# Moving three gain multiplies and the last-key transposes in the first batch, and respacing batch 1's attention bursts, in a fused attention and feed-forward kernel

## Chip, cores and metric

One core of a Trainium2 chip. The time is the device time of one launch in microseconds (us), lower is better. All runs quoted are fast, with a granted TensorE clock of 0.998 to 1.0. Kernels are compared only with the kernel before in the same rounds on the same chip.

## The reference

```python
def _attn_ref(q, k, v):                      # q, k, v: (8, 12, 448, 64)
    scores = 1/sqrt(64) * q @ k.transpose
    attn = np.maximum(scores, 0.0) ** 2 / 448
    return attn @ v

def _moe_ref(x, g_ln, w_ch1, w_ch2):         # x: (8, 448, 768)
    xn = (x - mean(x)) / sqrt(var(x) + 1e-6) * g_ln
    return x + np.maximum(xn @ w_ch1, 0.0) @ w_ch2      # 768 -> 3072 -> 768
```

Eight batches; 12 heads in 6 pairs per batch, so pairs 0 to 5 are batch 0, 6 to 11 batch 1, 12 to 17 batch 2. The output of attention, transposed, is x.

## The kernel before

TensorE does everything large. A batch's first layer has 24 column blocks of 128; in between them, "bursts" compute three score tiles of the next batch each. The first batch has no earlier first layer to hide in, so its attention runs on its own (`step_fine`), in a pipeline of TensorE (scores), ScalarE (relu out of PSUM), VectorE (square, evictions).

The variance need not be applied before the first layer (it is a factor per token, put in at the end), but the mean must: `xc = x*g - mean*g`. The `ones` matrix holds -1/768, so the mean product gives -mean.

```python
    def av_out(i, ps, evac_by):              # eviction of one pair's attention-value product
        b, pr = divmod(i, NPAIR)
        ...
            nc.vector.tensor_scalar(xT_of(b, pr), ps, c2, None, op0=Alu.mult)          # L362
        ...
        if b == 0:
            if pr < GAIN_FIRST:              # GAIN_FIRST = 3
                nc.vector.tensor_scalar(xc[:, pr, :], xT_of(b, pr), g_sb[:, pr:pr + 1],
                                        None, op0=Alu.mult)                            # L367, the gain multiply
        elif pr == 1: ...                    # sums for the later batches' mean

    def step_fine(i):                        # two pairs of batch 0, i and i + 1
        att_QK(i, 0)                         # scores (L293), then relu on ScalarE (L303)
        att_T(i + 1)                         # transposes of q, k (L229), copy (L268)
        att_square(i, 0)                     # VectorE (L306)
        att_QK(i, 1)
        att_square(i, 1)
        ...warm_up(3)...                     # i == 0 only; products that keep TensorE busy (L600)
        att_QK(i, 2)
        ...
            first_last_keys()                # i == 0: transposes of the last 64 keys of pairs 0, 1; copies (L275)
            warm_up(2)
        att_square(i, 2)
        att_QK(i, NF)                        # last-key product of both pairs (L288)
        ...

    def first_end():                         # i = 6
        att_AV(i - 1, 0); att_QK(i, 0); att_QK(i, 1); att_AV(i - 1, 1)
        mean_part(i - 2)                     # L376
        att_T(i + 1, nc.scalar.copy, next_f())
        mean_part(i - 1)
        att_T(i + 2, nc.scalar.copy, ...)
        # then ffn_1_first: centering of xc 0..2 (L397), first-layer products (L719)

    V_AT = {21: 14, 23: 16}                  # value loads during batch 0's first layer (numbers put in)
    STATS_AT = {0: (18, 21, 23), 1: (10, 14, 17, 22), 2: (2, 5, 8, 14)}
    IN_SECOND = (3, 6, 9, 13, 16, 19, 21)    # column blocks of batch 1 that are followed by a burst

    def queued(i):                           # when pair i's scores are done
        if PE_T * NPAIR <= i + 3 < NP_ALL:
            att_T(i + 3)                     # from pair 12: transpose by DMA, queue SP (L253)
            if i + 6 < NP_ALL:
                loads.append(i + 6)          # its ring slot is reloaded, queue POOL (L169 to L171)
    def excursion(n, ...):                   # a burst
        flush_loads()                        # issues what is in loads
        ...                                  # attention-value products of a finished couple of pairs (L323, L346)
        ...                                  # n scores, relus, squares; queued() for pairs that ended

    # in the loop over column blocks, batch 1: after the third burst the output stores of batch 0's
    # second layer that were held back (L459, 8 DMAs) are issued
                    while ni > bursts[1] and held_stores:
                        held_stores.pop(0)()
```

POOL issues the loads (weights, queries and keys into a ring of three slots, values). SP issues DMA transposes of the ring into `qkT` and the output stores. Both are worked off in program order.

## Time and profile before

| | |
|---|---|
| time | 521.75 us, median of 3 (521.41 to 521.87) |
| profiled execution | span 520.2 us, clock 1.0 |
| TensorE matmul busy | 512.8 us, 99% |
| first batch's first-layer product starts | 29.72 us |
| its second layer starts | 68.73 us |
| last-key product of batch 1's fourth burst | 104.42 us |
| batch 1's second layer starts | 123.31 us |

Busy time on the page's table of engines (engine, busy us, share of the span, instructions):

```profile
PE 512.8 (99%) x5688; PEld 310.4 (60%) x5688; DVE 370.8 (71%) x658; ACT 276.9 (53%) x456; POOL 222.7 (43%) x255
```

The view of waits, TensorE only (who waited, for whom, total us, times, longest):

```profile
PE f L600 <- DVE w L103: 1.2, 1, 1.2
PE sc L288 <- ACT at L303: 0.6, 1, 0.6
PE f L323 <- DVE at L306: 0.4, 2, 0.3
PE f L323 <- DVE xT L362: 0.3, 1, 0.3
...
```

By both, TensorE has almost nothing to win. What they hide is time between starts that is not counted as a wait. The chain of waits (start us, us, what) of the first batch, followed back from the first-layer product:

```profile
10.84 0.63 DVE at L306
11.46 0.54 DVE qkT_t L268
...
13.69 0.58 DVE xc L367
...
16.98 0.60 DVE xc L367
...
20.81 0.40 DVE xc L367
...
27.08 0.55 DVE xT L362
...
27.67 0.35 PE f L376
28.02 0.63 PE f L229 x16
28.65 0.31 PE f L376
...
28.98 0.69 DVE xc L397
...
29.72 0.73 PE f L719 x3
```

For 17 us the chain stays inside VectorE, and three of its members are the gain multiplies (L367), which nobody needs before 28.98 us. ScalarE is close behind, as its relus in the timeline show (start, us, engine, line, operation, count, in brackets the idle time before and what ended it):

```profile
6.83 2.54 ACT L303 ACTIVATE at<-sc 128x896 bf16<-128x896 f32 x3 [0.46 <-PE sc L293]
9.89 9.27 ACT L303 ACTIVATE at<-sc 128x896 bf16<-128x896 f32 x11 [0.52 <-PE sc L288]
19.63 1.85 ACT L303 ACTIVATE at<-sc 128x896 bf16<-128x896 f32 x2 [0.47 <-PE sc L293]
21.73 4.36 ACT L303 ACTIVATE at<-sc 128x896 bf16<-128x896 f32 x5 [0.25 <-DVE at L306]
```

The timeline of TensorE at batch 1's sixth burst (first line: its four last-key products) and at its last burst:

```profile
114.27 0.36 PE L288 MATMUL sc<-qkT_t 64*64 64x448 bf16 x4
...
117.90 0.36 PE L323 MATMUL f<-at,v_ring 128*64 128x448 bf16 x2
118.55 0.38 PE L323 MATMUL f<-at,v_ring 128*64 128x448 bf16 x2 [0.29 <-DVE at L306]
119.09 0.57 PE L323 MATMUL f<-at,v_ring 128*64 128x448 bf16 x4 [0.16 <-DVE at L306]
119.59 0.55 PE L293 MATMUL sc<-qkT_t 64*128 64x448 bf16 x4
...
122.55 0.93 PE L323 MATMUL f<-at,v_ring 128*64 128x448 bf16 x8
123.31 0.98 PE L499 MATMUL f<-w,h 128*64 128x384 bf16 x10
```

Eight attention-value matmuls take 119.59 - 117.90 = 1.69 us from start to next start; three us later eight take 123.31 - 122.55 = 0.76. The bracketed waits add up to 0.45 only; starts show about twice that, because the modelled end of a matmul covers part of the idle time.

The SP queue around batch 1's middle bursts:

```profile
94.72 5.71 SPq L253 DMA_TRANSPOSE qkT_t<-qk_ring  x2
...
102.74 4.37 SPq L459 DMA_DIRECT2D out_dram<-acc_t  x4
107.50 5.26 SPq L253 DMA_TRANSPOSE qkT_t<-qk_ring  x2
```

The first of these is pair 15's transpose (landed 9.4 us after issue, at 104.1), the one at 107.50 is pair 17's (5.4 us, 112.9). These two are needed in the fourth and the sixth burst.

### The profile page before, as it was taken

The page shows a single profiled execution, that of the slowest core. Times are in us where ns is not written, and L with a number is a line of the kernel's source. Part 1 is how long each engine was busy: PE and PEld are TensorE (multiplying, and loading weights), DVE is VectorE, ACT ScalarE, POOL GpSimd, SP SyncE. Part 2 cuts the span into 40 slices and gives each one's busy share as a digit, 9 for nine tenths or more (in the row PEclk, how much of TensorE's full clock was granted, in tenths as well). Part 3 has the DMA queues.
Part 4 walks back from the last instruction along what each step waited for, and adds up shares of the span by engine and source line. Part 5 has one row for each costly group of instructions (what it writes and reads, how often), then busy time and mean ns, then how long its engine had stood idle before and what let it go on. Part 6 is the DMA issues. An engine that isn't in the chain of part 4 may idle for free.

```text
span 520.2 us, 13589 instructions
## 1 busy us (share of the span) xinstructions
PE 512.8 (99%) x5688; PEld 310.4 (60%) x5688; DVE 370.8 (71%) x658; ACT 276.9 (53%) x456; POOL 222.7 (43%) x255
## 2 busy tenths in 40 slices
PE   8999999999999999999999999999999999999996
PEld 4445566555765566655787556655666556665665
DVE  5966779878958769587685868787695866950255
ACT  6976642786247662476624766476524765234320
POOL 8727115688423853238632287238532000320031
PEclk9999999999999999999999999999999999999999
DMA  9999999999436992559934799369923300340022
GB/s 138 190 197 202 183 203 164 138 189 113 79 92 91 117 100 62 122 70 121 83 74 107 73 111 146 75 81 116 89 70 100 62 1 2 74 113 1 1 59 64
DMA packets 175245, 53.01 MB, mean 102 GB/s; under 512 B 154192, under 2 KB 175184, under 8 KB 175184
## 3 DMA queue, kind: packets, MB, share of 16 engines
q0 software_dynamic: 103680, 25.75, 54.5%
q1 hardware_dynamic: 70976, 26.03, 27.5%
q8 instruction: 44, 0.72, 0.6%
q10 hardware_dynamic: 528, 0.37, 0.2%
q14 instruction: 17, 0.14, 0.1%
HBM read 51.91 MB, written 11.01 MB: 121 GB/s over the span
## 4 chain that ended last, share of the span: by engine, by line
PE 93%; DVE 4%; ACT 2%; issue 0%
PE f L431 41%; PE f L499 34%; PE f L323 5%; PE sc L293 4%; PE f L482 3%; DVE at L306 2%; PE f L293 2%; ACT at L303 1%; PE sc L288 1%; PE f L346 1%; PE f L600 1%; PE f L719 1%; DVE xT L362 1%; PE f L229 1%; DVE qkT_t L268 1%; ACT h L433 0%
## 5 line engine op out<-in xcount | busy, mean ns | idle before, releaser
L431 PE MATMUL f<-xc,w 128*64 128x448 bf16 x2256 | 225.6, 353 | 0.1
L431 PEld LDWEIGHTS <-w 128*64 128x64 bf16 x2256 | 125.8, 110 | 91.8 <-issue 13.6
L433 ACT ACTIVATE h<-f 128x448 bf16<-128x448 f32 x188 | 102.7, 546 | 102.5 <-PE f L431 98.0
L499 PE MATMUL f<-w,s_sb 128*64 128x384 bf16 (+2 forms) x1584 | 130.0, 324 | 0.0
L499 PEld LDWEIGHTS <-s_sb 128*64 128x64 bf16 x1584 | 92.7, 110 | 34.4
L303 ACT ACTIVATE at<-sc 128x896 bf16<-128x896 f32 x120 | 103.2, 918 | 5.3 <-PE sc L293 4.4
L306 DVE TENSOR_TENSOR at<-at 128x896 bf16<-128x896 bf16 x168 | 95.5, 617 | 4.8 <-ACT at L303 4.6
L532 POOL TENSOR_TENSOR o_t<-o_t,x_tok 128x384 f32<-128x384 f32 x26 | 24.3, 936 | 149.4 <-ACT o_t L531 149.4
L169 POOL DMA_DIRECT2D qk_ring<-in_q_dram x36 | 46.1, 1282 | 85.6 <-DMA qkT_t<-qk_ring 60.3
L299 DVE TENSOR_SCALAR at<-f 128x448 bf16<-128x448 f32 x89 | 52.6, 619 | 30.7 <-PE f L293 30.7
L531 ACT ACTIVATE o_t<-f,rstd 128x384 f32<-128x384 f32 x26 | 15.1, 581 | 93.5 <-DVE acc_t L536 29.9
L493 DVE TENSOR_TENSOR s_sb<-h 128x1536 bf16<-128x1536 bf16 x65 | 64.1, 1002 | 0.0
L170 POOL DMA_DIRECT2D qk_ring<-in_k_dram x36 | 55.0, 1528 | 12.6 <-DMA w<-in_moe_w_ch_dram 12.6
L499 PE MATMUL f<-w,h 128*64 128x384 bf16 x624 | 52.9, 326 | 0.0
L171 POOL DMA_DIRECT2D qk_ring<-in_k_dram x36 | 46.6, 1294 | 6.4 <-DMA w<-in_moe_w_ch_dram 4.8
L499 PEld LDWEIGHTS <-h 128*64 128x64 bf16 x624 | 36.8, 110 | 14.2
L532 POOL TENSOR_TENSOR acc_t<-acc_t,x_tok 128x384 f32<-128x384 f32 x24 | 28.8, 1209 | 22.3 <-ACT acc_t L531 19.6
L323 PE MATMUL f<-at,v_ring 128*64 128x448 bf16 x288 | 36.5, 357 | 0.8 <-DVE at L306 0.4
L181 POOL DMA_DIRECT2D v_ring<-in_v_dram x36 | 32.8, 1218 | 0.0
L397 DVE SCALAR_TENSOR_TENSOR xc<-f,g_sb,xc 128x448 bf16<-128x448 f32 x45 | 28.5, 677 | 5.4 <-PE f L391 4.6
L362 DVE TENSOR_SCALAR xT<-f 128x448 bf16<-128x448 f32 x33 | 20.3, 617 | 14.3 <-PE f L323 11.3
L293 PE MATMUL sc<-qkT_t 64*128 64x448 bf16 x192 | 30.0, 356 | 0.2 <-DVE qkT_t L268 0.2
(86 smaller groups left out, 392.0 us busy)
## 6 DMA issues: line engine op xcount, KB each, us to landing
w<-in_moe_w_ch_dram POOLq DMA_DIRECT2D x6, 768.0 KB, 12.6
w<-in_moe_w_ch_dram POOLq DMA_DIRECT2D x4, 1152.0 KB, 29.3
v_ring<-in_v_dram POOLq DMA_DIRECT2D x21, 192.0 KB, 5.1
qk_ring<-in_q_dram POOLq DMA_DIRECT2D x36, 112.0 KB, 4.7
qk_ring<-in_k_dram POOLq DMA_DIRECT2D x36, 96.0 KB, 5.1
out_dram<-o_t SPq DMA_DIRECT2D x8, 168.0 KB, 2.2
out_dram<-acc_t SPq DMA_DIRECT2D x7, 168.0 KB, 2.2
out_dram<-o_t SPq DMA_DIRECT2D x8, 144.0 KB, 2.1
```

Of the source, the lines that this page charges most:

```text
L170: nc.gpsimd.dma_start(k_to[:, :NF], k[b, heads, :SF].rearrange("x (p t) d -> p t x d", t=NF))
L171: nc.gpsimd.dma_start(k_to[:SS, NF], k[b, 2 * a:2 * a + 2, SF:].rearrange("x s d -> s x d"))
L293: nc.tensor.matmul(by_j(half[hh]), k_of(i, r, t, P), q_of(i, r), start=True, stop=True)
L299: nc.vector.tensor_scalar(at[:, x], half[x], 0.0, None, op0=Alu.max)
L303: nc.scalar.activation(at, ps[:, :, :S], Act.Relu)
L306: nc.vector.tensor_mul(attn[i, t], attn[i, t], attn[i, t])
L323: nc.tensor.matmul(ps[hh * D:(hh + 1) * D, :], weights, values, start=start, stop=stop)
L431: nc.tensor.matmul(ps[c * D:(c + 1) * D, :], w1[:, ki, n0:n0 + D], xc[:, ki, :], start=(ki == 0), stop=(ki == K1 - 1))
L433: nc.scalar.activation(h[:, ni, CARRY:], ps, Act.Relu)
L493: nc.vector.tensor_tensor(s_sb[:, n], x, y, op=op)
L499: nc.tensor.matmul(ps[c * D:(c + 1) * D, :d1 - d0], stat[:, ki, c * D:(c + 1) * D], w2[:, slot, ki, d0:d1], start=(start and ki == 0), sto ...
L532: nc.gpsimd.tensor_tensor(o_t, o_t, x_half(m, dh), op=Alu.add)
```

## The change

The intent: take the gain multiplies out of VectorE's chain and do them where VectorE waits for the last mean product; bring the last-key product of the first pairs forward; give batch 1's last burst three column blocks of distance instead of two.

```diff
@@ av_out
         if b == 0:
-            if pr < GAIN_FIRST:
-                nc.vector.tensor_scalar(xc[:, pr, :], xT_of(b, pr), g_sb[:, pr:pr + 1], None, op0=Alu.mult)
-        elif pr == 1:
+            return
+        if pr == 1:
@@ step_fine
         att_QK(i, 1)
+        if i == 0:
+            first_last_keys()
         att_square(i, 1)
@@
         else:
-            first_last_keys()
-            warm_up(2)
+            warm_up(3)
@@ first_end
         att_AV(i - 1, 1)
+        att_T(i + 1, nc.scalar.copy, next_f())
         mean_part(i - 2)
-        att_T(i + 1, nc.scalar.copy, next_f())
         mean_part(i - 1)
+        for ki in range(GAIN_FIRST):
+            nc.vector.tensor_scalar(xc[:, ki, :], xT_of(0, ki), g_sb[:, ki:ki + 1], None, op0=Alu.mult)
         att_T(i + 2, nc.scalar.copy, sc_turn.items[-1][:, 0])
@@
-    STATS_AT = {0: (18, 21, 23), 1: (10, 14, 17, 22), 2: (2, 5, 8, 14)}
-    IN_SECOND = (3, 6, 9, 13, 16, 19, 21)
+    STATS_AT = {0: (18, 21, 23), 1: (10, 16, 19, 22), 2: (2, 5, 8, 14)}
+    IN_SECOND = (3, 6, 9, 13, 15, 18, 21)
```

## The prediction

> **What bounds the kernel.** TensorE: the table of engines gives matmuls 512.8 of 520.2 us, granted clock 1.0; the list of waits gives TensorE only 2.9 us. The Trainium skill ("Perfetto Trace Analysis", opening note) calls matmul busy time a bad metric for pipelined matmuls; this trace agrees, since lost time hides inside "busy" groups, so I read starts in the timeline. From 42 us on TensorE runs nearly back to back. Two places lose time:
>
> 1. First batch's attention, 9 to 30 us. The chain of waits runs through VectorE almost without a gap from 10.84 to 27.62 us, and holds three gain multiplies (0.58, 0.60, 0.40 = 1.58 us). ScalarE is nearly full too: relus without a break from 9.89 to 19.16 us, then idle 0.47 and 0.25 until 26.09. Before that, the first last-key product waits for its copies (9.13 us), starts at 9.37, and leaves ScalarE idle 0.52 us.
> 2. Batch 1's last burst, two column blocks after the one before. Its 8 attention-value matmuls take 117.90 to 119.59 = 1.69 us; elsewhere eight take 0.75. Loss 0.94 us, to VectorE's squares.
>
> **What the change does.**
> - Last-key transposes one square earlier: copies at about 8.5 us, product at about 8.9, relu at about 9.4, 0.5 us earlier. The added warm-up matmul fills idle time. The keys land at 7.6 us (3.2 + 4.4), close to the new use at 7.5: may cost 0.1 to 0.2.
> - Gains out of VectorE's chain: up to 1.5 us there, but ScalarE then limits: its last relu can end about 1.2 us earlier (0.52 + 0.47 + 0.25).
> - Gains put back behind the last eviction, 0.33 to 0.5 us each, 1.0 to 1.3 us, of which 0.8 was idle waiting for the mean. VectorE, not the mean, then releases the centering. Net, the first-layer product starts 0.8 to 1.3 us earlier (before: 29.72).
> - Batch 1's bursts at 13, 15, 18, 21: three blocks before the last, and the short gap where no attention-value product follows. The 0.94 us stall should vanish.
>
> **How much survives.** The early microsecond meets a DMA chain that computation does not pace: second-layer weights land at 79.3 us (needed at about 80.6), release the ring's last query/key load, then transposes in one queue. Pair 15's is issued at 94.72, lands 9.4 us later, at 104.1; its product starts at 104.4 to 104.6. So only about 0.3 us of slack is left: I expect TensorE to arrive early and wait 0.5 to 0.9 us there. The next (pair 17, 107.50 + 5.4 = 112.9) is also needed near 113. Gain: 0.94 + about 0.3 = about 1.2 us.
>
> **Predicted: 520.5 us, 8 in 10 between 519.6 and 521.2.** Faster by over 2%: 0.005; within 2%: 0.99; slower by over 2%: 0.005.
>
> **Signs.** Right: last-key product near 8.9 us; no gain multiply before 26 us, three in a row behind the last eviction; first-layer product near 28.6 us; a new TensorE wait on pair 15's transpose just before 105 us, after which the shift is only about 0.3 us; batch 1's last burst's eight matmuls in 0.75 us; everything after it about 1.2 us early. Wrong: first-layer product at 29.5 us or later; a stall at block 15 or 18.
>
> **What would make it wrong.** If transposes move earlier with computation, the gain reaches 2.1 us. If the gains take over 0.5 us each, or pair 17's transpose stalls the moved burst, it falls to 0.5. DMA landings are of one profiled run, and may move by half a microsecond.

## The result, and the profile after

Measured: 520.97 us, median of 4 (519.58 to 521.56), against 521.81 us, median of 4, of the kernel before. The ratio is 0.9981, 95% interval 0.9960 to 1.0002; a ratio is the mean time of one kernel's fast runs over that of the other's of the same rounds, so it is not quite the ratio of the medians. In five further rounds of the same kernel (below) it was 0.9971 (0.9959 to 0.9983). So the change gains 1.0 to 1.5 us of 522, well within 2%. The first interval includes 1 and the second does not: that there is a gain at all rests on the repeat. The profiled execution took 520.69 us (before: 521.98).

In the lines of after, source lines have moved by one or two (L431 is L430, L499 is L498, L719 is L721), and the multiplies are L708. Engines and TensorE's waits:

```profile
PE 511.8 (99%) x5689; PEld 306.5 (59%) x5689; DVE 370.4 (71%) x658; ACT 276.8 (53%) x456; POOL 222.6 (43%) x255
```

```profile
PE f L599 <- DVE w L103: 1.2, 1, 1.2
PE sc L288 <- DMA qkT_t<-qk_ring: 0.8, 1, 0.8
PE f L229 <- DMA w<-in_k_dram: 0.4, 1, 0.4
PE f L229 <- DVE xT L362: 0.2, 1, 0.2
```

The waits for other engines (L303, L306) are gone, and two waits for DMAs have come. The timeline of the first batch: ScalarE's relus, and VectorE's and TensorE's end of the stage.

```profile
6.83 1.73 ACT L303 ACTIVATE at<-sc 128x896 bf16<-128x896 f32 x2 [0.46 <-PE sc L293]
9.03 15.86 ACT L303 ACTIVATE at<-sc 128x896 bf16<-128x896 f32 x19 [0.47 <-PE sc L293]
```

```profile
25.46 1.18 DVE L362 TENSOR_SCALAR xT<-f 128x448 bf16<-128x448 f32 x2
26.56 0.82 DVE L708 TENSOR_SCALAR xc<-xT,g_sb 128x448 bf16<-128x448 bf16 x3
27.36 1.87 DVE L396 SCALAR_TENSOR_TENSOR xc<-f,g_sb,xc 128x448 bf16<-128x448 f32 x3
```

```profile
8.01 0.25 PE L229 MATMUL f<-identity,w 64*64 64x64 bf16 x4 [0.43 <-DMA w<-in_k_dram]
...
9.35 0.38 PE L288 MATMUL sc<-qkT_t 64*64 64x448 bf16 x4
...
28.10 0.73 PE L721 MATMUL f<-xc,w 128*128 128x448 bf16 x3
```

The 19 relus from the third on now run without a break, and the last ends at 24.90 instead of 26.09 us. The three multiplies stand in a row behind the last eviction and take 0.82 us together. The first-layer product starts at 28.10 instead of 29.72: 1.62 us earlier. The last-key product is not earlier (9.35, before 9.37): its transposes waited for the load of the keys.

TensorE at the sixth and seventh burst of batch 1, and the SP queue that serves it:

```profile
111.53 0.35 PE L288 MATMUL sc<-qkT_t 64*64 64x448 bf16 x2
112.73 0.38 PE L288 MATMUL sc<-qkT_t 64*64 64x448 bf16 x2 [0.85 <-DMA qkT_t<-qk_ring]
113.04 0.36 PE L293 MATMUL sc<-qkT_t 64*128 64x448 bf16 x2
...
117.52 0.92 PE L323 MATMUL f<-at,v_ring 128*64 128x448 bf16 x8
118.38 0.55 PE L293 MATMUL sc<-qkT_t 64*128 64x448 bf16 x4
```

```profile
94.37 5.36 SPq L253 DMA_TRANSPOSE qkT_t<-qk_ring  x2
...
101.99 2.73 SPq L458 DMA_DIRECT2D out_dram<-acc_t  x4
105.50 5.70 SPq L253 DMA_TRANSPOSE qkT_t<-qk_ring  x2
```

The last burst's eight matmuls take 0.86 us instead of 1.69: that stall is gone. In its place the four last-key products of the sixth burst are torn apart. The first two are of pair 16, the other two of pair 17, and pair 17's transpose, issued at 105.50, landed 7.2 us later, at 112.7.

The kernel between these places runs at a fixed pace, so marks in the timeline give an exact account. From the mark at batch 1's second layer to the end it is 396.9 us before and 396.8 after.

| us | before | after | difference |
|---|---|---|---|
| start to first-layer product | 29.72 | 28.10 | -1.62 |
| from there to the fourth burst's last-key product (104.42, 102.82) | 74.70 | 74.72 | +0.02 |
| from there to batch 1's second layer (123.31, 122.10) | 18.89 | 19.28 | +0.39 |
| rest of the span | 396.9 | 396.8 | -0.1 |

So 1.62 us won in the first batch arrive in full at the fourth burst, and the third line, where the respacing should win about 0.9, loses 0.4.

### The profile page after: what moved, and what is told of

Its sections match the earlier page's. It is cut to its first block, busy times and chain, and to the rows that moved or that the text cites. A ratio compares the mean times of both kernels' runs of the same rounds, so it can differ in the third digit from the quotient of the medians.

```text
span 518.9 us, 13591 instructions
## 1 busy us (share of the span) xinstructions
PE 511.8 (99%) x5689; PEld 306.5 (59%) x5689; DVE 370.4 (71%) x658; ACT 276.8 (53%) x456; POOL 222.6 (43%) x255
## 4 chain that ended last, share of the span: by engine, by line
PE 91%; DVE 3%; DMA 2%; ACT 2%; POOL 0%; issue 0%; POOLq 0%; ACTq 0%
PE f L430 40%; PE f L498 34%; PE f L323 5%; PE sc L293 4%; PE f L481 3%; PE f L293 2%; DVE at L306 1%; ACT at L303 1%; DMA qkT_t<-qk_ring 1%; PE sc L288 1%; DMA w<-in_k_dram 1%; PE f L346 1%; PE f L721 1%; DVE xT L362 1%; DVE qkT_t L268 0%; ACT h L432 0%
## 5 line engine op out<-in xcount | busy, mean ns | idle before, releaser
L430 PE MATMUL f<-xc,w 128*64 128x448 bf16 x2256 | 225.5, 353 | 0.1
L430 PEld LDWEIGHTS <-w 128*64 128x64 bf16 x2256 | 125.9, 110 | 91.6 <-issue 13.6
L432 ACT ACTIVATE h<-f 128x448 bf16<-128x448 f32 x188 | 102.8, 547 | 102.5 <-PE f L430 97.6
L498 PE MATMUL f<-w,s_sb 128*64 128x384 bf16 (+2 forms) x1584 | 130.0, 324 | 0.0
L498 PEld LDWEIGHTS <-s_sb 128*64 128x64 bf16 x1584 | 90.0, 110 | 37.2
L303 ACT ACTIVATE at<-sc 128x896 bf16<-128x896 f32 x120 | 102.8, 918 | 5.1 <-PE sc L293 4.2
L306 DVE TENSOR_TENSOR at<-at 128x896 bf16<-128x896 bf16 x168 | 95.6, 618 | 4.9 <-ACT at L303 4.7
L498 PE MATMUL f<-w,h 128*64 128x384 bf16 x624 | 52.9, 326 | 0.0
L498 PEld LDWEIGHTS <-h 128*64 128x64 bf16 x624 | 35.7, 110 | 15.3
```

Of the source, the lines that this page charges most:

```text
L303: nc.scalar.activation(at, ps[:, :, :S], Act.Relu)
L306: nc.vector.tensor_mul(attn[i, t], attn[i, t], attn[i, t])
L430: nc.tensor.matmul(ps[c * D:(c + 1) * D, :], w1[:, ki, n0:n0 + D], xc[:, ki, :], start=(ki == 0), stop=(ki == K1 - 1))
L432: nc.scalar.activation(h[:, ni, CARRY:], ps, Act.Relu)
L498: nc.tensor.matmul(ps[c * D:(c + 1) * D, :d1 - d0], stat[:, ki, c * D:(c + 1) * D], w2[:, slot, ki, d0:d1], start=(start and ki == 0), sto ...
```

## The experiments

Theory T, formed from this: TensorE comes early to batch 1, and there meets DMA landings that computation does not pace; the sixth burst, moved one block up, is the one that hits pair 17's. Its main rivals: the wait in that one profile is an accident and the parts simply add; or the wait is the respacing's own doing.

Twelve runs were made, in three groups of four on three chips, 5 rounds each (c_bursts has six executions); all gave correct results. Times and ratios against before of the same rounds, and the marks of each profile:

| run | time, us | ratio (95%) | first-layer product | to 4th burst | to 2nd layer of batch 1 |
|---|---|---|---|---|---|
| before (first profile) | | | 29.72 | 74.70 | 18.89 |
| after (first profile) | | | 28.10 | 74.72 | 19.28 |
| a_after | 520.35 | 0.9971 (0.9959-0.9983) | 28.46 | 75.15 | 18.22 |
| b_first | 520.74 | 0.9977 (0.9965-0.9989) | 27.98 | 74.72 | 19.04 |
| c_bursts | 520.67 | 0.9984 (0.9971-0.9997) | 29.15 | 74.70 | 18.07 |
| d_loads | 520.31 | 0.9975 (0.9962-0.9988) | 27.78 | 75.18 | 18.29 |
| d_both | 519.93 | 0.9963 (0.9950-0.9975) | 28.45 | 74.94 | 18.07 |
| e_gain | 521.26 | 0.9987 (0.9975-1.0000) | 28.18 | 75.43 | 18.89 |
| f_keys | 522.07 | 1.0005 (0.9992-1.0019) | 29.59 | 74.70 | 18.88 |
| g_split | 520.76 | 0.9978 (0.9966-0.9991) | 28.94 | 74.91 | 18.06 |
| d_both_2 | 520.95 | 0.9971 (0.9958-0.9983) | 28.66 | 75.70 | 18.06 |
| h_nokeys | 520.82 | 0.9969 (0.9956-0.9981) | 28.15 | 75.44 | 18.07 |
| d_stores | 520.03 | 0.9956 (0.9944-0.9969) | 28.27 | 74.90 | 18.06 |
| b_first_both | 521.64 | 0.9983 (0.9969-0.9996) | 29.55 | 74.76 | 18.88 |

Read the last two columns first. Undisturbed, "to 4th burst" is 74.70 to 74.72 in every profile, and "to 2nd layer" is 18.88 or 18.89 with the old places of the bursts and 18.06 or 18.07 with the new ones. What stands above is a wait. For "to 4th burst" it is always the same one: laid product by product beside an undisturbed profile, each of the nine others loses its excess at the first product of batch 0's second layer that needs the last quarter of that layer's weights, and this product starts 0.04 us after these weights land. In the profile after (landed 78.96) and in b_first (78.83) it also starts 0.04 us after the landing, but nothing is lost yet. So in all eleven profiles with the moved multiplies TensorE has caught up with this landing; in the three without, the product starts 1.28 us (before), 0.41 (c_bursts) and 0.38 us (f_keys) after it. The column of first-layer products is not as steady: kernels with the same first-batch code differ by up to 0.6 us (before 29.72, c_bursts 29.15), and those with the whole new code by more.

### a_after: the change once more

No edit.

> The change as it is, once more, beside its parts. Theory T (first-batch part brings TensorE 1.6 us early to batch 1; there the sixth burst, moved one block up, waits for the transpose of pair 17, whose load sits behind value loads in one queue): gain about 1.2 us over before (ratio 0.9977), with a TensorE wait of 0.5 to 1.5 us inside the four last-key products of the sixth burst, and more scatter from run to run than before, since a DMA landing now sets the pace. Rival R (the two parts act in different places, their gains simply add, the wait seen once is an accident of that run): ratio 0.9953 (2.5 us), no such wait in most runs.

The gain was 0.0029 x 522 = 1.5 us. The expected wait in the sixth burst was a miss: here it is 0.16 us (18.22 - 18.06). Pair 17's transpose landed at 112.4, and TensorE came 0.8 us later than in the first profile. It had lost that elsewhere: 1.2 us of wait for the last keys' load at 8.40 us, and 0.3 for the second layer's last weights. So which landing TensorE waits for changes from run to run. The scatter of the five runs (0.8 us) was not larger than that of the eleven of before (1.4 us), against T.

### b_first: the first batch's part alone

```diff
-    STATS_AT = {..., 1: (10, 16, 19, 22), ...}
-    IN_SECOND = (3, 6, 9, 13, 15, 18, 21)
+    STATS_AT = {..., 1: (10, 14, 17, 22), ...}
+    IN_SECOND = (3, 6, 9, 13, 16, 19, 21)
```

> First-batch part alone (gains moved, last keys early); bursts of batch 1 at their old places. T: first-layer product at about 28.1 us as in the whole change; the sixth burst comes one block (1.18 us) later than in the whole change, so it meets pair 17's transpose at most 0.3 us too early; the last burst's 8 attention-value matmuls lose about 0.9 us as before. Gain 1.3 to 1.6 us, ratio about 0.997: as much as the whole change, so the respacing adds about nothing to it. R (gains add): 1.6 us here, 2.5 for the whole. Second rival (the respacing carries the gain, the early time is absorbed): gain under 0.5 us.

Gain 0.0023 x 522 = 1.2 us, first-layer product 27.98. The sixth burst met pair 17's transpose (landed 112.6) 0.15 us too early (19.04 - 18.89), and the last burst's eight matmuls took 1.68 us as before. As T said: without the respacing most of the early time survives, because the sixth burst is one block later.

### c_bursts: the respacing alone

The reverse: the kernel before, with the new `STATS_AT` and `IN_SECOND`.

> Respacing alone; first batch as before. T: TensorE is not early, so the sixth burst reaches its last-key products at about 113.1 us, pair 17's transpose lands at 112.5 to 112.9: wait at most 0.3 us; the last burst's eight matmuls take 0.75 instead of 1.69 us. Gain 0.7 to 0.9 us, ratio about 0.9984. Rival (the wait is the respacing's own doing, whatever comes before it): a wait of about 1 us in the sixth burst here too, gain about 0.

Gain 0.0016 x 522 = 0.8 us, and 18.07 in the last column: no wait in the sixth burst (its four products 0.30 us; pair 17 landed at 112.51, its product started at 112.57). The rival falls: a wait of about 1 us is not the respacing's own, it takes both parts. But only 0.06 us was to spare, so a later landing would have been waited for here too. The parts alone give 1.2 + 0.8 = 2.0 us, the whole 1.0 to 1.5. Each of these gains is known to 0.6 us or worse, so that the whole is less than the sum of its parts is shown by the marks of the first profile, not by these times.

### d_loads: pair 17's load ahead of two value loads

Pair 17's queries and keys were loaded behind two value loads, of pairs 14 to 17, that are needed no sooner (with the order turned, this run lists no wait for values).

```diff
             if b == 0 and ni in V_AT:
+                flush_loads()
                 load_v(V_AT[ni])
```

> The whole change, and pair 17's query/key load issued ahead of the two value loads (a flush of held loads before each of them). T: that load lands 4 to 6 us earlier (near 100 us, not 105.3); its transpose then starts behind the output stores, at about 105 us instead of 105.5, and lands 0.3 to 1.5 us earlier: wait down from 1.0 to 0 to 0.7 us, gain over before 1.6 to 2.3 us. Rival (the transpose is slow because of what runs beside it, 7.2 us against 5.4, not late): starts earlier but lands at about the same time, wait stays near 1 us, gain 1.2.

The load landed at 101.8 instead of 105.3, but the transpose was issued only at 106.28, right behind the output stores of the same queue (last ended 106.11). Wait in the sixth burst 0.23 us (18.29 - 18.06); gain 0.0025 x 522 = 1.3 us, below the expected 1.6. So two things held the transpose: its load, and the stores queued ahead of it. Taking one away leaves the other. It was not the number of stores: the queue's view of waits shows that the last of them stood 2.0 us for a transpose, and it was issued at 105.79, when pair 16's landed (105.77). So, in the queue's order, pair 17's transpose stood behind the landing of pair 16's.

### d_both: also the stores behind the transpose

```diff
-                    while ni > bursts[1] and held_stores:
+                    while ni >= bursts[3 if b == 1 else 1] and held_stores:
```

on top of d_loads.

> The whole change, pair 17's load ahead of the value loads, and the first batch's 8 output stores queued behind pair 17's transpose instead of ahead of it. In the run with the early load alone, that load landed at 101.8 us, but the transpose was issued only at 106.28, right behind the stores. T: now it is issued when its buffer is free, 103.3 to 104.5 us, and lands at 108.5 to 111: no wait in the sixth burst, and the whole first-batch gain comes through: 2.2 to 2.6 us over before, ratio 0.9950 to 0.9958. Rival (the early time is lost somewhere else anyway): ratio stays at 0.997 to 0.9975.

The SP queue of this kernel, then TensorE at its sixth burst:

```profile
94.82 10.51 SPq L253 DMA_TRANSPOSE qkT_t<-qk_ring  x3
105.42 1.94 SPq L458 DMA_DIRECT2D out_dram<-o_t  x4
```

```profile
112.11 0.36 PE L288 MATMUL sc<-qkT_t 64*64 64x448 bf16 x4
```

Pair 17's transpose is now the third of the group of three: issued at 104.1, before pair 16's landed (105.2), landed at 109.3, 2.8 us before its use at 112.1. No wait, 18.07. Gain 0.0037 x 522 = 1.9 us, less than the 2.2 to 2.6 expected; in its profile the first-layer product came at 28.45, and 0.24 us went at the second layer's last weights.

### e_gain: only the gain multiplies moved

The change with the last keys, warm-ups and bursts at their old places.

> Only the gain multiplies moved (with the two mean products behind the transposes); last keys and bursts as before. T: last-key product at about 9.4 us as before; the three multiplies leave VectorE's chain; first-layer product 0.5 to 0.9 us earlier than before (28.6 to 29.2 us in a run where before has 29.72). At the end a gain of 0.5 to 0.9 us, ratio about 0.9987, since so little earlier arrival just fits the slack of the transposes. Rival (last keys are the whole gain): first-layer product within 0.3 us of before, ratio 1.000.

First-layer product 28.18: as early as with everything. So the multiplies carry the first batch's gain. (This kernel also has the mean products behind the transposes, which no run takes apart; but the last eviction, which stands before them, already ends at 26.73 us instead of 28.18, and that is 1.45 of the 1.54 us.) Of the 1.5 us, 0.73 were lost before the fourth burst (75.43), and the TensorE timeline shows where:

```profile
72.25 6.99 PE L481 MATMUL f<-w,h 128*64 128x384 bf16 x84
79.79 4.09 PE L481 MATMUL f<-w,h 128*64 128x384 bf16 x48 [0.55 <-DMA w<-in_moe_w_ch_dram]
```

These are batch 0's second layer; the matmuls from 79.79 on need the last quarter of its weights, which were issued at 42.8 and landed 37.0 us later, at 79.8. In the kernel before they landed at 79.3 and were needed at about 80.6, and its matmuls ran through:

```profile
73.79 10.89 PE L482 MATMUL f<-w,h 128*64 128x384 bf16 x132
```

Coming 1.5 us early turns the 1.3 us of slack into a wait. Gain at the end 0.0013 x 522 = 0.7 us.

### f_keys: only the last keys early

The change with the multiplies and mean products back in their old places, and the old bursts.

> Only the last-key transposes ahead of the square (and the added warm-up product). T: last-key product at 8.9 to 9.4 us, depending on when the keys land (7.5 to 8.3 us in the runs so far); VectorE, with its three multiplies, stays the chain of this stage, but starts it up to 0.5 us earlier: first-layer product 0.2 to 0.5 us earlier, ratio 0.9990 to 0.9997. Rival (VectorE's total limits, an earlier start is lost in it): no shift of the first-layer product, ratio 1.000.

Ratio 1.0005: no gain. The last-key product came at 9.22 and the first-layer product at 29.59, within the scatter of the two profiles with the old code (29.72, 29.15). Moreover the next transposes then waited 0.3 us for their own keys at 11.00. The rival's forecast holds; its reason, that VectorE's total limits while the multiplies are in it, fits but is not shown apart.

### g_split: a smaller first piece of the last keys

On top of d_both:

```diff
-        load_heads(0, [("q", 2, 2), ("k", 2, 2), ("k last", 0, H), ("q", 4, 4), ("k", 4, 4), ("v", 0, 4),
+        load_heads(0, [("q", 2, 2), ("k", 2, 2), ("k last", 0, 4), ("q", 4, 4), ("k", 4, 4), ("k last", 4, 8), ("v", 0, 4),
```

> As d_both, and the load of the last keys split: heads 0 to 3 first, the other eight after the next query and key loads. T (the early transposes wait for a load that lands only just in time, 0.4 to 1.2 us of wait in three of four profiles): first piece lands 0.3 to 0.8 us earlier, no wait before the last-key transposes, last-key product at 8.9 us or earlier in every profile, and 0.1 to 0.5 us faster than d_both with less scatter. Rival: the extra load delays the next queries and keys, and what is won at 8 us is lost at 10 us: same as d_both.

The piece landed 2.7 us after issue instead of 3.9 to 5.1, and the last-key product came at 8.71, the earliest of all. But the first-layer product came at 28.94, and TensorE waited 0.7 us for a copy of later transposes and 0.5 us for values. Time 520.76 against 519.93 of d_both beside it: what was won is lost, as the rival said, and more. Its last second-layer weights also came later, at 80.0 us against 79.5.

### d_both_2, h_nokeys, d_stores, b_first_both: which mends count

d_both_2 is d_both again. h_nokeys is d_both with the last keys back in their old place. d_stores is the change with the stores behind the transpose and without the early load. b_first_both is d_both with the old places of the bursts.

> The kernel with the early load and the late stores once more, as the yardstick for the three beside it. T: about 2 us over before (ratio 0.996), no wait in the sixth burst.

Gain 0.0029 x 522 = 1.5 us, again without a wait in the sixth burst (18.06; transpose landed at 110.9, used at 113.1). But this profile lost 1.0 us in the second layer at its last weights (issued at 43.1, landed 37.4 us later, at 80.5) and 0.6 us at 10.9 us waiting for the keys of pairs 2 and 3.

> The same without the early last keys (transposes of the last keys and two warm-up products back in their old place). T: in the profiles so far the first-layer product came at 28.18 us with the gains moved alone, and at 27.78 to 28.46 us with both; so the early keys are worth 0 to 0.3 us, and this kernel is within 0.3 us of its neighbour, with no wait for the last keys' load. Rival (the early keys do carry part of the gain): 0.5 us slower or more.

Ratio 0.9969 against 0.9971 beside it, first-layer product 28.15 with the last-key product at 9.35. The early keys are worth nothing measurable.

> The whole change with the output stores behind pair 17's transpose, but its load in its old place. T: the load lands at about 105.3 us as before, so the transpose is issued at about 105.5 and lands at 111 to 112.7 us; needed at about 111.7: wait of 0 to 1 us in the sixth burst, time between the whole change and the kernel with both mends. Rival (the stores alone were what kept the transpose back): issued before 104.5, no wait, as fast as the kernel with both mends.

The fastest kernel: 520.03 us, ratio 0.9956 (gain 2.3 us), with no wait in the sixth burst. As T said, the load landed at 105.7 and the transpose was issued at 105.8, no earlier than in the change (105.50); it landed at 111.6 and was needed at 111.9. So this order does not make the transpose earlier; whether moving the stores away made it land sooner (5.8 us after issue instead of 7.2), or that was chance, is open: without the stores moved it took 5.7 us in a_after and 5.6 in d_loads too. That it is faster than d_both is not established either: the intervals overlap, and its profile lost 0.2 us at the weights where d_both_2's lost 1.0.

> Early load and late stores, gains and keys moved, but the bursts of batch 1 at their old places. T: with pair 17 out of the way, the respacing is worth its own 0.8 us: the last burst's eight matmuls take about 1.6 us again, and this kernel is 0.7 to 0.9 us slower than its neighbour with the new places. Rival (respacing only helped by chance): same time as its neighbour.

Slower than d_both_2 by (0.9983 - 0.9971) x 522 = 0.6 us by the ratios and 0.7 by the medians, with 18.88 against 18.06 in the last column: the respacing is worth 0.82 us, what c_bursts showed, once pair 17 does not stand in the way. Its first-layer product was late (29.55) because the transposes of pair 2 waited 0.7 us for queries and 0.6 us for keys. That cost nothing against its neighbour: the last weights landed at 80.44 us here and at 80.49 there, and both reached the fourth burst at 104.3 to 104.4.

## Why the prediction was right or wrong

The size was right: 1.2 us predicted, 0.8 by the medians and 1.0 by the ratio at first, 1.5 in the repeat, and the time lies inside the range. Point by point:

- **VectorE's chain as the limit of the first batch, with ScalarE close behind: right.** e_gain shows it by itself: moving the multiplies alone brings the first-layer product to 28.18. The last relu ends 1.19 us earlier, as the predicted 1.2.
- **The first-layer product 0.8 to 1.3 us earlier: 1.62 between the first two profiles.** The term that was mis-sized is the three multiplies put back, predicted at 0.33 to 0.5 us each, 1.0 to 1.3 together, and measured at 0.82 in a row: each does last 0.33, but the next starts 0.25 after it. With that, the centering follows the last eviction by 0.72 us instead of 0.81, where 0.2 to 0.5 had been deducted. The rest is that the last eviction ends 1.54 us earlier (26.64 against 28.18) and not only the relus' 1.2: before, VectorE had lagged behind the last relu. In the profile before the multiplies lasted 0.58, 0.60 and 0.40. In c_bursts and f_keys, which have the same old code, all three took 0.34 to 0.39; against c_bursts (29.15) the first-layer product comes only 1.05 us earlier, inside the forecast. The Trainium skill ("VectorE: DVE Perf Modes", "What auto-detection actually checks") says that a one-source operation with 16-bit operands in SBUF can run in the fastest mode, and its section "Why PSUM operands drop a tier" gives a 32-bit PSUM source only the plain rate. The trace agrees: 0.25 us from start to start in a row, against 0.55 for the eviction of equal shape from 32-bit PSUM (at 27.08). The same page's cycle table ("Side-by-side": elements over 4, 8 to fill, about 150 to start, at 0.96 GHz) would have given an estimate of (112 + 8 + 150) / 0.96 = 281 ns, nearer to the 0.33 us than the trace of before. What the long ones have in common is on POOL:

```profile
13.38 0.79 POOL L150 DMA_DIRECT2D w<-in_k_dram  x1
```

```profile
13.69 0.58 DVE L367 TENSOR_SCALAR xc<-xT,g_sb 128x448 bf16<-128x448 bf16 x1
```

The fourteen profiles hold 42 of these multiplies, and seven lasted over 0.34 us, all with the old code. Each of the seven began while POOL was in a DMA issue that ran on for another 0.28 to 0.53 us, and ended 0.07 to 0.10 us after it; for the other 35, any issue under way at the start was over within 0.11 us. So the change also moved the multiplies to a place where POOL issues nothing. No run kept POOL quiet at the old place, so this is a coincidence seen seven times in seven, not an experiment.
- **Last keys 0.5 us earlier: wrong.** Landing at 7.6 us was read from one profile as costing 0.1 to 0.2; the landings were 7.1 to 8.4 us in the runs with early keys that have the undivided load. And where the product did come early (8.86 in d_both_2), the next loads were waited for instead. f_keys and h_nokeys: nothing gained.
- **The stall of 0.94 us in the last burst vanishes: right**, sized from starts rather than bracketed waits; the segment gives 0.82 (18.88 to 18.06).
- **The early time is lost at pair 15's transpose before 105 us, leaving a shift of 0.3 us: this step was wrong.** The shift at 102.8 us was still 1.60. Pair 15's transpose landed at 101.7, not 104.1. The 9.4 us from issue to landing in the profile before is the longest among the fourteen; the others show 6.6 to 8.1. The mechanism (TensorE arrives before a DMA that computation does not pace) was right, but it works at two other places: pair 17's transpose, which cost 1.2 us in the first profile after (19.28 - 18.06) and about 0.2 in three others, and the last weights of batch 0's second layer: the stretch to the fourth burst is 0.4 to 1.0 us longer in a_after, d_loads, e_gain, h_nokeys and d_both_2, and each of these lists that wait. (d_both, d_stores and g_split lose 0.2 us at the same product without a listed wait.) The prediction named both numbers (79.3 against 80.6; 112.9 against "near 113") but took only the smallest slack as the wall. With 1.6 us of early arrival every slack below that is a wall, and which one holds depends on the landings of the run.

That the sum came out right is therefore partly luck: in the first profile the wait expected at pair 15 was absent, the one at pair 17 was larger than thought, and the weights happened to land 0.38 us earlier than in before (78.96 against 79.34), just early enough to let all 1.62 us through. Pair 17's wait was mended (d_both: none in two profiles, with the transpose landing 2.1 to 2.8 us before its use). An earlier landing of the weights was not tried; with the multiplies moved, TensorE waits for it or just meets it in every profile.

The Trainium skill ("DMA: Bandwidth & Descriptors", "Issuing engines are not separate DMA queues") says that DMAs started by different engines run on the same 16 engines and interleave. This fits pair 17's transpose on SP taking 4.4 to 7.2 us to land while POOL's loads are under way; no run here took the loads away to show it.

## What to carry to other kernels

When a change makes an early stage faster, list every later DMA landing with its slack, not only the one with the smallest, and take the landing times from several executions: here slacks of 1 to 2 us stood against landings that move by more than that. Two correct improvements can add up to less than their sum when the second moves a consumer ahead of a transfer that the first has already caught up with. And cut the timeline into segments between fixed marks: they repeated to 0.02 us here, while whole times scattered by 2 us, and each excess in a segment named its wait.

## What the Trainium skill lacked or had wrong

- "DMA: Bandwidth & Descriptors" gives the bandwidth of a DMA transpose, but no landing time of a single one beside other traffic. Pair 15's transpose, the same in all fourteen profiles, landed 6.6 to 9.4 us after its issue, pair 17's 4.4 to 7.2.
- "Perfetto Trace Analysis" ("Identifying the Most-Contended Engine") looks for the engine with the highest use, for TensorE by its arithmetic rate and its share of weight loads. The weight loads took 60% before and 59% after, and matmul busy time 99% in both; where the 1.3 us between the two spans were lost, only the starts show. Slack of landings against first use is on no page.
- "VectorE: DVE Perf Modes": the estimate of 281 ns from its cycle table is below what the traces show for the gain multiply, 325 to 338 ns in the 35 that no long DMA issue on POOL overlapped.
